# The prologue of a fused attention and gated-product kernel in another order

## The chip, the cores and the metric

One core of one Trainium2 chip runs the kernel. A core has a TensorE (PE: matrix products, into PSUM), a VectorE (DVE), a ScalarE (ACT), a GpSimd (POOL) and a SyncE (SP), each with an instruction queue of its own that it works through in order; SP, ACT and POOL also issue DMA transfers, which run on 16 DMA engines that the core's queues share. The metric is device time in microseconds (us); lower is better. Before the change the median of three runs is 641.73 us (639.29 to 646.2).

## The reference

x has 2048 rows of 576. Everything is bfloat16 at the ends.

```python
mod = (_silu(c) @ w_mod).reshape(c.shape[0], 6, 1, -1)
sa, ca, ga, sb, cb, gb = (mod[:, 0], mod[:, 1], mod[:, 2], mod[:, 3], mod[:, 4], mod[:, 5])
h = _layernorm(x) * (1 + ca) + sa
x = x + ga * A(h, A_wqkv, A_wo)
h = _layernorm(x) * (1 + cb) + sb
x = x + gb * B(h, B_w_gate, B_w_up, B_w_down)
```

A is attention with 32 heads of 18 columns. Row s attends to 8 rows only: s, s-2, ..., s-14 (rows before the first are masked). Its steps are q, k, v = h @ wqkv; 8 logits per row and head; a softmax over these 8; the weighted sum of 8 rows of v; and the product with wo. B is (h @ w_gate) * (h @ w_up) @ w_down with an inner width of 4608.

## The kernel before

The 2048 rows are cut into eight chunks of 256 (CH), each of two tiles of 128 rows (ST = 2, index j). The attention of a chunk i is a list of small pieces, which are Python functions that issue instructions:

- A(i): `a_ln` (layer norm of x, and loads of the next chunks of x), `a_t` (transposes through PE, then scale and shift into hT, by ACT and DVE in turns), five `a_q` (two column tiles of q or k each, products into PSUM, then copied by ACT to qT or kT), two `a_v` (product for v, copied by ACT to v_sb, then stored to vd, a buffer in DRAM, by a DMA that ACT issues, L322).
- B_log(i): eight `b_p` (DVE: q times k shifted by 2w rows, into prod, L341; three buffers) and eight `b_l` (PE: sum per head, into the PSUM tile lg, L351), then `b_sm`, the softmax (DVE, with one exponential on ACT, L367; its result is attn).
- B_av(i): `b_ld` (POOL issues a gather of v's eight shifted copies from vd into vsh, 1.15 MB for a tile of 128 rows, L333), `b_mul` twice per tile (DVE: vsh times attn, L383) and `b_add` (DVE: the sum over the eight, o_sb).
- B_out(i): `b_o` (transposes of o_sb, copied by ACT to oT), `b_w` twice (product pw with wo, L415, then DVE: times ga, plus x), `b_ln`, `b_t` (the second layer norm and its transposes, h2T).

Behind the prologue, `gate_up` and `down` run over five groups of chunks ([0], [1], [2, 3], [4, 5], [6, 7]). The gate and up products (L485, L492) of the first group begin when chunk 0's h2T is there; the attention of the later chunks is spread between them as background pieces.

PE's instructions stay in the order in which the program issues them (`manual_schedule`). The order on DVE, ACT, POOL and SP is chosen by a scheduler at build time, which follows the program's order and priorities; once chosen it is fixed, and each engine waits at its next instruction until its operands are there. Loads on SP and ACT take one of eight semaphores in turn, and a transfer waits at its issue until the one that had the same semaphore has landed.

The prologue before: x's chunk 0, the modulation weights wmA, wqk, wv_raw, x's chunk 1, wmB on SP; c, the four pieces of wo and the zero rows ahead of vd on ACT. Then layer norm 0, the modulation columns for the first norm (pm, written to modc), a reorder of wv's columns by POOL (L558), all of A(0), the loads of wmC and of two blocks of gate and up weights, and

```python
    do(zip_lists(A(1), B_log(0)))
    mod_columns(wmB, 1, True)
    mod_row(wmC, 0, ga_bc)
    mod_row(wmC, 1, gb_bc)
    ...
    do(zip_lists(A2[:7], B_av(0)))
    o0 = B_out(0)
    do(o0[:4], A2[7:], o0[4:])
```

zip_lists takes one piece from each list in turn. The first three blocks of w_down (wd) are loaded by POOL in between.

Of the kernel before, what the change touches and what calls it, by code (L numbers as in the profile page):

```python
# [7 lines left out]
BF = mybir.dt.bfloat16  # L8
# [19 lines left out]
HALO = 16  # L28
# [12 lines left out]
def kernel(  # L41
# [13 lines left out]
    nc = tc.nc  # L55
# [13 lines left out]
    xres = pool("xres", 4)  # L69
# [19 lines left out]
    def ps(shape, dt, name):  # L89
        return psp.tile(shape, dt, name=name, tag="bank")  # L90
# [13 lines left out]
    vd = dramp.tile([HALO + S, D], BF, name="vd")  # L104
# [6 lines left out]
    def load_rows(i, pl, name):  # L111
        ts = []
        for j in range(ST):
            xt = pl.tile([P, D], BF, name=name)
            nc.sync.dma_start(xt[:], x_flat[i * CH + j * P: i * CH + (j + 1) * P, :])
            ts.append(xt)
        return ts

    x_in, x_res = {}, {}

    def load_x(i):
        if i < NCH and i not in x_in:
            x_in[i] = load_rows(i, xin, "x_t")

    def load_res(i):
        x_res[i] = load_rows(i, xres, "x_r")

    wgu_blk, wd_blk = {}, {}
    NG = len(GROUPS)
# [2 lines left out]
    def load_wgu(g):  # L132


        if g >= NG * NBLK or g in wgu_blk:
            return
        cs = slice((g % NBLK) * NB, (g % NBLK + 1) * NB)
        wb = wgup.tile([P, KF, 2, NB], BF, name="wgu")
        wr = wgup.tile([P, NB], BF, name="wgr")
        for t, wsrc in enumerate((B_w_gate, B_w_up)):  # L140
            nc.sync.dma_start(wb[:, :, t, :], wsrc[0:KF * P, cs].rearrange("(k p) n -> p k n", p=P))
            nc.sync.dma_start(wr[64 * t:64 * (t + 1), :], wsrc[KF * P:D, cs])
        wgu_blk[g] = (wb, wr)

    def load_wd(g):
        if g >= NG * NBLK or g in wd_blk:
            return
        r0 = (g % NBLK) * FB * P
        wb = wdp.tile([P, FB, D], BF, name="wd")
        nc.gpsimd.dma_start(wb[:], B_w_down[r0:r0 + FB * P, :].rearrange("(k p) n -> p k n", p=P))  # L150
        wd_blk[g] = wb

    load_x(0)
# [1 line left out]
    sp = sp_guard.__enter__()  # L155
# [6 lines left out]
    def load_wm(blks):  # L162
        wm = sp.tile([P, KT, 2, DP], BF, name="wm", bufs=2)
        nc.gpsimd.memset(wm[:, :, :, D:], 0.0)
        nc.gpsimd.memset(wm[64:, KF, :, :], 0.0)
        for bi, blk in enumerate(blks):
            nc.sync.dma_start(wm[:, 0:KF, bi, 0:D], w_mod[0:KF * P, blk * D:(blk + 1) * D].rearrange("(k p) n -> p k n", p=P))
            nc.sync.dma_start(wm[0:64, KF, bi, 0:D], w_mod[KF * P:D, blk * D:(blk + 1) * D])
        return wm

    wmA = load_wm((0, 1))
    nc.gpsimd.memset(ind[:], 1.0)
    nc.gpsimd.affine_select(out=ind[:], in_=ind[:], compare_op=ALU.is_ge, fill=0.0, base=0,
                            pattern=[[P, KT], [-DH, H]], channel_multiplier=1)
# [9 lines left out]
    nc.gpsimd.memset(wv_raw[64:, KF, :], 0.0)  # L184
    nc.sync.dma_start(wv_raw[:, 0:KF, :], A_wqkv[0:KF * P, 2 * D:3 * D].rearrange("(k p) n -> p k n", p=P))
    nc.sync.dma_start(wv_raw[0:64, KF, :], A_wqkv[KF * P:D, 2 * D:3 * D])
    load_x(1)
    wmB = load_wm((3, 4))
    nc.gpsimd.memset(wo[64:, KF, :], 0.0)
    for dd4 in range(4):  # L190

        nk = (DH - dd4 + 3) // 4
        wsrc = bass.AP(A_wo.tensor, A_wo.offset + dd4 * D, [[DH * D, H], [4 * D, nk], [1, D]])
        nc.scalar.dma_start(wo[dd4 * H:(dd4 + 1) * H, 0:nk, :], wsrc)
    nc.scalar.dma_start(vd[0:HALO, :], wqk[64:64 + HALO, KF, 0, 0:D])


    c_f = sp.tile([P, KT], F32, name="c_f")
    nc.vector.tensor_copy(c_f[:], c_bf[:])
# [8 lines left out]
    def mod_columns(wm, pi, dup):  # L208
        if dup:
            nc.gpsimd.tensor_copy(wm[:, :, :, D:DP], wm[:, :, :, D - 64:D])  # L210
        pm = ps([P, 2, KT], F32, "pm")
        for bi in range(2):
            for m in range(KT):
                for kt in range(KT):
                    nc.tensor.matmul(pm[:, bi, m:m + 1], lhsT=wm[:, kt, bi, m * P:(m + 1) * P],
                                     rhs=sc[:, kt:kt + 1], start=(kt == 0), stop=(kt == KT - 1))
        nc.vector.tensor_copy(modc[:, 2 * pi, :], pm[:, 0, :])
        nc.vector.tensor_scalar_add(modc[:, 2 * pi + 1, :], pm[:, 1, :], 1.0)

# [90 lines left out]
    def a_v(i, j):  # L310
        hT = aa[i]["hT"]
        pv = ps([P, 512], F32, "pv")
        pvr = ps([P, 64], F32, "pvr")
        for kt in range(KT):
            nc.tensor.matmul(pv[:], lhsT=hT[:, kt, j * P:(j + 1) * P], rhs=wv[:, kt, 0:512], start=(kt == 0), stop=(kt == KT - 1))  # L315
        for kt in range(KT):
            nc.tensor.matmul(pvr[:], lhsT=hT[:, kt, j * P:(j + 1) * P], rhs=wv[:, kt, 512:D], start=(kt == 0), stop=(kt == KT - 1))
        v_sb = vstage.tile([P, D], BF, name="v_sb")
        nc.scalar.copy(v_sb[:, 0:512], pv[:])
        nc.scalar.copy(v_sb[:, 512:D], pvr[:])  # L320
        r0 = HALO + i * CH + j * P
        nc.scalar.dma_start(vd[r0:r0 + P, :], v_sb[:])  # L322

    def A(i):
        return ([lambda: a_ln(i), lambda: a_t(i)] + [lambda g=g: a_q(i, g) for g in range(5)]
                + [lambda j=j: a_v(i, j) for j in range(ST)])
# [9 lines left out]
    def b_p(i, w):  # L336

        b = bb.setdefault(i, dict(prod={}, vsh={}))
        off = HALO - DIL * (W - 1 - w)
        prod = prodp.tile([P, KT, CH], BF, name="prod")  # L340
        nc.vector.tensor_tensor(prod[:], aa[i]["qT"][:], aa[i]["kT"][:, :, off:off + CH], ALU.mult)  # L341
        b["prod"][w] = prod

    def b_l(i, w):
        b = bb[i]
        if w == 0:
            b["lg"] = ps([P, ST, W, H], F32, "lg")
        prod = b["prod"].pop(w)
        for j in range(ST):
            for m in range(KT):  # L350
                nc.tensor.matmul(b["lg"][:, j, w, :], lhsT=prod[:, m, j * P:(j + 1) * P], rhs=ind[:, m, :],  # L351
                                 start=(m == 0), stop=(m == KT - 1))
# [23 lines left out]
    def b_ld(i, j):  # L376
        bb[i]["vsh"][j] = b_vsh(i, j)

    def b_mul(i, j, hf):
        b = bb[i]  # L380
        v = b["vsh"][j][:, 4 * hf:4 * hf + 4]
        at = b["attn"][:, j, 4 * hf:4 * hf + 4, None, :].to_broadcast([P, 4, DH, H])
        nc.vector.tensor_tensor(v, v, at, ALU.mult)  # L383
# [52 lines left out]
    def B_log(i):  # L436
        r = [lambda: b_p(i, 0), lambda: b_p(i, 1)]
        for w in range(W):
            r.append(lambda w=w: b_l(i, w))
            if w + 2 < W:  # L440
                r.append(lambda w=w: b_p(i, w + 2))
        return r + [lambda: b_sm(i)]

    def B_av(i):
        r = [lambda: b_ld(i, 0)]
        for j in range(ST):
            if j + 1 < ST:
# [92 lines left out]
    def do(*lists):  # L540
        for ls in lists:
            for piece in ls:
                piece()

    def zip_lists(a, b):
        r = []
        while a or b:
            if a:
                r.append(a.pop(0))
            if b:  # L550
                r.append(b.pop(0))
        return r
# [4 lines left out]
    for kt in range(KT):  # L557
        nc.gpsimd.tensor_copy(wv[:, kt, :].rearrange("p (d h) -> p d h", d=DH),  # L558
                              wv_raw[:, kt, :].rearrange("p (h d) -> p d h", d=DH))
    do(A(0)[1:])  # L560
    nc.vector.tensor_copy(sc_bc[:], sc[:, :, None].to_broadcast([P, KT, P]))
    wmC = load_wm((2, 5))
    load_wgu(0)
    load_wgu(1)
    do(zip_lists(A(1), B_log(0)))
    mod_columns(wmB, 1, True)
    mod_row(wmC, 0, ga_bc)
    mod_row(wmC, 1, gb_bc)
    sp_guard.__exit__(None, None, None)
    hhp = pool("hhp", 1)  # L570
    load_wgu(2)
    for g in range(3):
        load_wd(g)
    A2 = A(2)
    do(zip_lists(A2[:7], B_av(0)))
    o0 = B_out(0)
    do(o0[:4], A2[7:], o0[4:])

    gbg = {0: B_log(1) + B_av(1),
           1: B_av(2) + B_log(3),  # L580
# [40 lines left out]
```

## Time and profile before

| | us |
|---|---|
| median of three runs | 641.73 |
| lowest and highest run | 639.29, 646.2 |
| span of the profiled execution (its own time from first to last instruction) | 640.6 |
| PE busy in it | 576.0 (90%) |
| DVE busy | 303.3 (47%) |
| ACT busy | 283.3 (44%) |
| POOL busy | 77.3 (12%) |
| first gate/up product starts | 81.75 |

The span is one execution, taken by the profiler; it lies within the runs' spread. Matrix products are pipelined, so that PE's busy time isn't PE at its peak. A DMA share near 1 says that all 16 DMA engines had work throughout a stretch. In the lists of transfers the time to landing runs from the issue to the last byte's arrival: in the prologue the two gathers of vsh for chunk 0 took 10.0 and 12.0, the v stores of chunk 0 took 7.0 and 7.5.

### The profile page before, as it was taken

How to read it: one execution, taken by the hardware profiler on the slowest of the kernel's cores; microseconds unless marked ns; L12 is line 12 of the kernel's file. 1: busy time of each engine (PE TensorE's matmuls, PEld its weight loads, DVE VectorE, ACT ScalarE, POOL GpSimd, SP SyncE). 2: the span in 40 equal slices, each digit the busy share in tenths (PEclk: the TensorE clock that was granted, in tenths of full speed). 3: DMA queues.
4: the chain of work that ended last, by engine and by line, in shares of the span. 5: the costliest groups of instructions: out<-in, count | busy, mean ns of one | idle time of the engine just before them, and what ended most of it. 6: DMA issues, size and time to landing. Idle time of an engine off the chain costs nothing.

```text
span 640.6 us, 11591 instructions
## 1 busy us (share of the span) xinstructions
PE 576.0 (90%) x4604; PEld 318.6 (50%) x4672; DVE 303.3 (47%) x632; ACT 283.3 (44%) x582; POOL 77.3 (12%) x128
## 2 busy tenths in 40 slices
PE   1786589989989789999999988999999989999996
PEld 1464267755667556444445654444445543333452
DVE  2547535945944933458385132458393331222103
ACT  2624366551556336455564432455552315555200
POOL 5710200022100222001001210001001110000010
PEclk9988779999999899999999999999999999999999
DMA  9994438886898356545644363446544344441151
GB/s 244 317 376 128 184 117 259 291 280 205 268 344 259 119 182 232 171 134 186 211 144 159 109 224 112 130 148 198 196 136 145 111 150 150 139 138 47 43 150 68
DMA packets 81575, 115.36 MB, mean 180 GB/s; under 512 B 5856, under 2 KB 71664, under 8 KB 81520
## 3 DMA queue, kind: packets, MB, share of 16 engines
q1 hardware_dynamic: 67104, 66.15, 33.2%
q0 software_dynamic: 10832, 45.42, 21.1%
q10 hardware_dynamic: 3584, 3.04, 1.5%
q8 instruction: 36, 0.59, 0.4%
q14 instruction: 19, 0.16, 0.1%
HBM read 109.86 MB, written 4.74 MB: 179 GB/s over the span
## 4 chain that ended last, share of the span: by engine, by line
PE 73%; DVE 10%; DMA 8%; issue 3%; ACT 2%; POOL 2%; SPq 1%; ACTq 0%; POOLq 0%; DVEq 0%
PE pg L492 19%; PE pu L492 18%; PE acc L516 15%; PE pg L485 6%; PE pq L300 4%; PE accr L517 3%; PE pw L415 3%; PE lg L351 2%; DMA wgu<-in_B_w_gate_dram 2%; DMA wgu<-in_B_w_up_dram 2%; PE pv L315 2%; DVE ln_stats L236 2%; DVE vsh L383 2%; DMA wm<-in_w_mod_dram 1%; DVE o_t L534 1%
## 5 line engine op out<-in xcount | busy, mean ns | idle before, releaser
L492 PEld LDWEIGHTS <-wgu 128*128 128x128 bf16 x1440 | 132.3, 98 | 125.8 <-issue 31.6
L492 PE MATMUL pu<-h2T,wgu 128*128 128x512 bf16 (+1 forms) x719 | 154.8, 338 | 1.9 <-DMA wgu<-in_B_w_up_dram 1.8
L492 PE MATMUL pg<-h2T,wgu 128*128 128x512 bf16 (+1 forms) x694 | 152.0, 338 | 3.0 <-issue 2.2
L516 PE MATMUL acc<-wd,hh 128*128 128x512 bf16 x541 | 147.6, 381 | 1.8 <-DMA wd<-in_B_w_down_dram 1.8
L497 ACT CAST g_sb<-pg 128x512 bf16<-128x512 f32 (+1 forms) x180 | 90.0, 500 | 112.1 <-PE pg L492 97.4
L517 PE MATMUL accr<-wd,hh 128*128 128x64 bf16 x576 | 111.1, 193 | 10.7 <-DVE o_t L535 8.7
L499 DVE TENSOR_TENSOR hh<-g_sb,u_sb 128x512 bf16<-128x512 bf16 (+1 forms) x180 | 65.8, 368 | 106.9 <-ACT u_sb L498 106.9
L498 ACT CAST u_sb<-pu 128x512 bf16<-128x512 f32 (+1 forms) x180 | 90.2, 501 | 42.7 <-PE pu L492 36.4
L516 PEld LDWEIGHTS <-hh 128*128 128x128 bf16 x576 | 56.4, 98 | 70.7 <-issue 12.4
L341 DVE TENSOR_TENSOR prod<-qT,kT 128x1280 bf16<-128x1280 bf16 x64 | 52.4, 828 | 53.3 <-PE lg L351 48.2
L300 PE MATMUL pq<-hT,wqk 128*128 128x256 bf16 x400 | 58.0, 292 | 19.2 <-DVE hT L264 9.8
L150 POOL DMA_DIRECT2D wd<-in_B_w_down_dram x45 | 33.9, 754 | 243.9 <-PE accr L517 238.4
L517 PEld LDWEIGHTS <-hh 128*128 128x128 bf16 x576 | 56.4, 98 | 2.6 <-issue 1.9
L300 PEld LDWEIGHTS <-wqk 128*128 128x128 bf16 x400 | 40.2, 104 | 33.4 <-issue 22.0
L485 PE MATMUL pg<-h2T,wgr 64*128 64x512 bf16 (+1 forms) x180 | 46.9, 341 | 1.7 <-ACT h2T L266 1.7
L485 PE MATMUL pu<-h2T,wgr 64*128 64x512 bf16 (+1 forms) x180 | 46.9, 341 | 0.0
L383 DVE TENSOR_TENSOR vsh<-vsh,attn 128x2304 bf16<-128x2304 bf16 x32 | 42.8, 1351 | 0.1
L534 DVE TENSOR_TENSOR o_t<-acc,gb_bc 128x512 bf16<-128x512 f32 x16 | 11.0, 687 | 47.6 <-PE accr L517 45.7
L333 POOL DMA_DIRECT2D vsh<-vd x16 | 14.2, 887 | 156.0 <-DVE o_sb L394 89.4
L264 DVE TENSOR_SCALAR h2T<-tr_pA,modc 128x256 bf16<-128x256 bf16 x16 | 6.6, 410 | 54.3 <-ACT h2T L266 54.3
L351 PEld LDWEIGHTS <-prod 128*128 128x128 bf16 x640 | 23.8, 96 | 9.0 <-DVE prod L341 0.9
L419 DVE TENSOR_TENSOR x<-pw,ga_bc 128x512 bf16<-128x512 f32 x16 | 10.8, 678 | 31.4 <-PE pw L415 31.4
(99 smaller groups left out, 446.1 us busy)
## 6 DMA issues: line engine op xcount, KB each, us to landing
wd<-in_B_w_down_dram POOLq DMA_DIRECT2D x45, 576.0 KB, 4.3
wgu<-in_B_w_gate_dram SPq DMA_DIRECT2D x45, 512.0 KB, 3.8
wgu<-in_B_w_up_dram SPq DMA_DIRECT2D x45, 512.0 KB, 4.9
vsh<-vd POOLq DMA_DIRECT2D x16, 1152.0 KB, 9.2
wm<-in_w_mod_dram SPq DMA_DIRECT2D x6, 576.0 KB, 7.2
wgr<-in_B_w_gate_dram SPq DMA_DIRECT2D x45, 64.0 KB, 3.0
wgr<-in_B_w_up_dram SPq DMA_DIRECT2D x45, 64.0 KB, 2.7
x_t<-in_A_x_dram SPq DMA_DIRECT2D x16, 144.0 KB, 4.3
```

The lines of the kernel that those rows point to most:

```text
L150: nc.gpsimd.dma_start(wb[:], B_w_down[r0:r0 + FB * P, :].rearrange("(k p) n -> p k n", p=P))
L300: nc.tensor.matmul(pq[:, gi, :], lhsT=wqk[:, kt, t, m * P:(m + 1) * P], rhs=hT[:, kt, :], start=(kt == 0), stop=(kt == KT - 1))
L341: nc.vector.tensor_tensor(prod[:], aa[i]["qT"][:], aa[i]["kT"][:, :, off:off + CH], ALU.mult)
L351: nc.tensor.matmul(b["lg"][:, j, w, :], lhsT=prod[:, m, j * P:(j + 1) * P], rhs=ind[:, m, :], start=(m == 0), stop=(m == KT - 1))
L383: nc.vector.tensor_tensor(v, v, at, ALU.mult)
L485: nc.tensor.matmul(pgu[f][t][:, 0:N], lhsT=wr[rows, cs], rhs=ht[rows, KF, 0:N], start=True, stop=False, skip_group_check=True)
L492: nc.tensor.matmul(pgu[f][t][:, 0:N], lhsT=wb[:, k, t, cs], rhs=ht[:, k, 0:N], start=False, stop=(k == KF - 1), skip_group_check=True)
L497: nc.scalar.copy(g[:, 0:N], pg[:, 0:N])
L498: nc.scalar.copy(u[:, 0:N], pu[:, 0:N])
L499: nc.vector.tensor_tensor(hh[:, f, 0:N], g[:, 0:N], u[:, 0:N], ALU.mult)
L516: nc.tensor.matmul(acc[j][:], lhsT=h, rhs=wb[:, f % FB, 0:512], start=(f == 0), stop=(f == FT - 1))
L517: nc.tensor.matmul(accr[:, j, :], lhsT=h, rhs=wb[:, f % FB, 512:D], start=(f == 0 and j == 0), stop=(f == FT - 1), skip_group_check=True)
```

## The change

All of it lies in the prologue; the groups of gate, up and down are left as they are.

- x's chunk 1 is loaded right behind wmA, ahead of wqk. wmB, which was loaded behind x's chunk 1, follows layer norm 1 (and so the loads of x's chunks 2 and 3). wo moves from ACT's queue to SP's, behind wmB; wmC follows wo.
- The zero rows ahead of vd come from a small tile of zeros, stored by SP, and not from wqk's zero part by ACT.
- Chunk 0's logits are put right behind its QKV: the first two b_l between its two a_v, and chunk 1's transposes and its first four a_q between the later b_l. The softmax follows, then the rest of A(1), layer norm 2, and b_mul, b_add of chunk 0, interleaved with chunk 2's transposes and a_q.
- Chunk 0's two v stores are issued by POOL instead of ACT.
- The three first wd blocks are loaded by SP instead of POOL; chunk 0's x for the residual is loaded earlier.
- At the end of the prologue one a_v of chunk 2 stands between b_o and b_w of chunk 0.

```diff
     def load_res(i):
-        x_res[i] = load_rows(i, xres, "x_r")
+        if i not in x_res:
+            x_res[i] = load_rows(i, xres, "x_r")
...
     wmA = load_wm((0, 1))
+    load_x(1)
...
-    load_x(1)
-    wmB = load_wm((3, 4))
     nc.gpsimd.memset(wo[64:, KF, :], 0.0)
-    for dd4 in range(4):
-
-        nk = (DH - dd4 + 3) // 4
-        wsrc = bass.AP(A_wo.tensor, A_wo.offset + dd4 * D, [[DH * D, H], [4 * D, nk], [1, D]])
-        nc.scalar.dma_start(wo[dd4 * H:(dd4 + 1) * H, 0:nk, :], wsrc)
-    nc.scalar.dma_start(vd[0:HALO, :], wqk[64:64 + HALO, KF, 0, 0:D])
-
+
+    def load_wo():
+        for dd4 in range(4):
+
+            nk = (DH - dd4 + 3) // 4
+            wsrc = bass.AP(A_wo.tensor, A_wo.offset + dd4 * D, [[DH * D, H], [4 * D, nk], [1, D]])
+            nc.sync.dma_start(wo[dd4 * H:(dd4 + 1) * H, 0:nk, :], wsrc)
+
+    zrow = sp.tile([HALO, D], BF, name="zrow")
+    nc.gpsimd.memset(zrow[:], 0.0)
+    nc.sync.dma_start(vd[0:HALO, :], zrow[:])
...
-        nc.scalar.dma_start(vd[r0:r0 + P, :], v_sb[:])
+        (nc.gpsimd if i == 0 else nc.scalar).dma_start(vd[r0:r0 + P, :], v_sb[:])
...
-    do(A(0)[1:])
+    A0, A1, A2 = A(0), A(1), A(2)
+    do(A0[1:7])
+    A1[0]()
+    wmB = load_wm((3, 4))
     nc.vector.tensor_copy(sc_bc[:], sc[:, :, None].to_broadcast([P, KT, P]))
+    L, PR = (lambda w: b_l(0, w)), (lambda w: b_p(0, w))
+    PR(0)
+    PR(1)
+    A0[7]()
+    L(0)
+    PR(2)
+    A0[8]()
+    b_ld(0, 0)
+    b_ld(0, 1)
+    for w, piece in ((1, None), (2, A1[1]), (3, None), (4, A1[2]), (5, A1[3]), (6, A1[4]), (7, A1[5])):
+        L(w)
+        if w + 2 < W:
+            PR(w + 2)
+        if piece:
+            piece()
+    b_sm(0)
+    load_wo()
     wmC = load_wm((2, 5))
+    do(A1[6:])
+    A2[0]()
+    load_res(0)
+    av = [lambda j=j, k=k: (b_mul(0, j, k) if k < 2 else b_add(0, j)) for j in range(ST) for k in range(3)]
+    av[0]()
     load_wgu(0)
     load_wgu(1)
-    do(zip_lists(A(1), B_log(0)))
     mod_columns(wmB, 1, True)
+    av[1]()
     mod_row(wmC, 0, ga_bc)
     mod_row(wmC, 1, gb_bc)
     sp_guard.__exit__(None, None, None)
     hhp = pool("hhp", 1)
     load_wgu(2)
+    do(zip_lists(av[2:], A2[1:7]))
     for g in range(3):
-        load_wd(g)
-    A2 = A(2)
-    do(zip_lists(A2[:7], B_av(0)))
+        load_wd(g, nc.sync)
     o0 = B_out(0)
-    do(o0[:4], A2[7:], o0[4:])
+    do(o0[:1], A2[7:8], o0[1:4], A2[8:], o0[4:])
```

(load_wd has a new parameter for the queue that issues it, GpSimd by default.)

More of the change, by code (lines that the diff above doesn't have):

```diff
@@ L143, in load_wgu, with load_wd @@
         wgu_blk[g] = (wb, wr)
-    def load_wd(g):
+    def load_wd(g, queue=nc.gpsimd):
         if g >= NG * NBLK or g in wd_blk:
@@ L149, in load_wd @@
         wb = wdp.tile([P, FB, D], BF, name="wd")
-        nc.gpsimd.dma_start(wb[:], B_w_down[r0:r0 + FB * P, :].rearrange("(k p) n -> p k n", p=P))
+        queue.dma_start(wb[:], B_w_down[r0:r0 + FB * P, :].rearrange("(k p) n -> p k n", p=P))
         wd_blk[g] = wb
```

## The prediction

> **What bounds the kernel now.** I read the page first: TensorE (PE) is busy 90% of the span, its gaps lie almost all in the first 82 us. The stage table shows that, each row being a stretch, the busy time of each engine (instruction counts in brackets), the granted PE clock, the busy share of the DMA engines and their rate:
>
> ```profile
> core 0: us, PE busy (x) PEld busy (x) DVE busy (x) ACT busy (x) POOL busy (x), PEclk, DMA share, GB/s
> 0.00:10.00 10.00, 0.00 (x0) 0.10 (x1) 2.40 (x9) 1.28 (x1) 8.79 (x20) 1.00 0.82 198
> ...
> 50.00:60.00 10.00, 5.58 (x39) 3.67 (x37) 6.90 (x9) 3.89 (x9) 0.00 (x0) 0.84 0.46 144
> 60.00:70.00 10.00, 5.99 (x46) 4.25 (x46) 6.34 (x8) 3.69 (x7) 3.73 (x5) 0.84 0.24 90
> ```
>
> Behind the prologue PE works 527.39 of 558 us, and the change leaves that part's instructions alone. So the question is one number: when the gate/up product (L485) starts. Then the timeline of the first 90 us (start, duration, engine line, idle time before it and what ended it):
>
> ```profile
> 12.39 0.21 ACT L201 ACTIVATE e_f<-c_f 128x5 f32<-128x5 f32 x1 [10.30 <-DMA wm<-in_w_mod_dram]
> ...
> 18.08 5.80 POOL L558 COPY wv<-wv_raw 128x576 bf16<-128x576 bf16 x5 [8.18 <-DMA wv_raw<-in_A_wqkv_dram]
> ...
> 19.89 6.62 PE L300 MATMUL pq<-hT,wqk 128*128 128x256 bf16 x47 [2.06 <-DVE hT L264]
> ...
> 27.23 2.48 DVE L341 TENSOR_TENSOR prod<-qT,kT 128x1280 bf16<-128x1280 bf16 x3 [1.16 <-ACT ln_rstd L240]
> ...
> 35.63 0.90 POOL L333 DMA_DIRECT2D vsh<-vd  x1 [5.38 <-DMA vd<-v_sb]
> ...
> 53.07 1.03 DVE L369 TENSOR_REDUCE ssum<-dd 128x64 f32<-128x512 f32 x1 [3.75 <-ACT dd L367]
> ...
> 56.48 3.89 DVE L383 TENSOR_TENSOR vsh<-vsh,attn 128x2304 bf16<-128x2304 bf16 x3
> 56.62 6.96 PE L300 MATMUL pq<-hT,wqk 128*128 128x256 bf16 x47 [0.18 <-DVE hT L264]
> ...
> 66.43 0.56 PE L405 MATMUL oT_pA<-ident,o_sb 128*128 128x128 bf16 x7 [0.93 <-DVE o_sb L394]
> ...
> 81.75 0.37 PE L485 MATMUL pg<-h2T,wgr 64*128 64x256 bf16 x1 [1.71 <-ACT h2T L266]
> ```
>
> To be seen: ScalarE (ACT) idles 10.30 us at the start, its queue standing behind the wo and vd transfers; chunk 0's softmax is late (3.75 us of it behind ACT, which stands at L322 until 48.12 and 51.11); the DMA engines are full from 10 to 50 us (share 1.06 to 1.09); the attention multiply L383 starts at 56.48 with both vsh tiles long there (issued 35.63 and 37.79, landed after 10.0 and 12.0).
>
> **The change, step by step.** All starts of the new kernel are estimates from these rows.
>
> *Start.* wo's four issues and vd's zero rows leave ACT, so e_f goes at about 5.6 and sc, which came 0.84 behind e_f (12.39 to 13.23), at 6.5. The modulation product waits for wmA instead: it landed at 11.9 beside 0.66 MB of wo; without it at 8.3 to 9.5 (1.6 MB at the 200 to 320 GB/s of these stretches). But DVE now has chunk 1's statistics (2.0 us and the small steps, x1 landing at 9 to 10) ahead of the modc copies: these come at 12 to 13 in place of 14.80, and ACT puts chunk 1's two ln_xn (0.87 each) among the hT steps. QKV of chunk 0 runs at full rate from about 15.3, not 19.89, and ends at 22, not 26.5. The zero rows' transfer on SP (18 KB) costs one issue, 0.5 us, under full DMA queues: nothing.
>
> *That gain is stopped at once.* kT's copies on ACT now stand behind chunk 2's ln_xn, which waits for a POOL memset, and POOL has the five wv copies ahead of it. wv_raw landed at 18.0 to 18.4; with 0.39 MB less ahead of it (wo and so on out, x1 in) 1.2 us earlier: 16.9 + 5.8 + 1.16 (wm memset) + 0.2 = 24.1, less up to 0.8 if the queue runs better. Then ACT needs 0.87 + 0.58 + 0.87 + 0.58: kT is whole at 26 to 27; I take 26.3, against 27.2. So logits start 0.9 us earlier, not 4.5.
>
> *Logits and softmax.* First product at 27.1. PE: lg 0.41, pv 1.35, two lg, transposes 0.8, two lg: 31.3; 1.6 for hT (it stood 1.78 there before); three pq groups of 1.4 and three lg: 38.3, where before lg ended at 45.5. Softmax: 0.83 + 1.01 + 0.69 + 0.64 + 1.03 + 0.54 + 0.68 = 5.4, two products of chunk 1 that are put between 1.6, handovers 0.6: attn at 46.0, against 56.1. ACT's exponential is ahead of the v stores here, so the 3.75 us go.
>
> *The added wait.* Chunk 0's two v stores move from ACT to POOL. Its order is: store 0, the wmB copy (wmB landed long before, at about 25), vsh0 (waits for store 0), **store 1**, vsh1 (waits for store 1). Store 1 is queued behind vsh0's wait, and its data behind vsh0's 1.15 MB on the same queue; in the old kernel both stores were out at 30.0. ACT's v_sb of chunk 1 waits for store 1 too, with ga_bc, gb_bc and chunk 2's hT behind it; those are not needed before 50.
> Prices: a store issued at 28.36 landed after 7.0, at 48.12 after 5.6, at 76 after 1.7 with idle queues. POOL's queue goes in order: wd landed at 33.8, 35.9, 38.0, then vsh0 7.6 us later and vsh1 4.2 later. Store 0: kT copy to 27.2, v_sb, issue 27.5, landed 32.5 to 35. vsh0 issued 33.5 to 36, landing 8.6 to 9.5 later (0.9 issue, some 1 to start, 7.6): 42 to 45. Store 1 lands 0.5 to 1.5 behind it. vsh1: 0.9 + 1 + 4.2 to 7.6: 48.5 to 56. I take 52, since SP's loads still run until about 50 and the full-queue rows are the nearest.
>
> The Trainium skill ("DMA: Bandwidth & Descriptors", section "Issuing engine by pattern") speaks against this move: a simple store belongs on Sync, and GpSimd's software path is the slower one. Its section on the anatomy of a software DMA gives about 2.0 us plus bytes over 436 GB/s, an estimate of 2.3 for a store and 4.7 for vsh; the chain would then end near 44 and bind nothing, and the sum would be that of the faster rival below. The full queues of this trace (7.0 us for such a store) decide otherwise.
>
> *What it moves.* Call T the start of the third multiply (vsh1's first). DVE's own chain allows 46.0 + 2 x 1.27 + 0.3 = 48.8; vsh1 makes it 52. DVE now has chunk 2's two hT steps behind it: 1.27 + 1.27 + 0.41 + 0.67 + 0.41 = 4.1, so chunk 2's QKV starts at T + 4.1 and not 56.6; 7.0 us to T + 11.1, where o_sb is ready (T + 8.9). Transposes 1.0, ACT's oT copies 1.4 with pv(2,0) on PE in their shade, pw's two big groups 4.1 (68.50 to 72.6): T + 17.6. From there to L485 it was 81.75 - 72.6 = 9.15 and stays so. Gate/up starts at T + 26.75: with 52 at 78.75, 3.0 us earlier. Old kernel by the same steps: QKV at 56.6, oT 2.8 us late for o_sb; that wait goes, too, and is in the sum.
>
> wd through SP and load_res earlier: nothing; wd is read first by the down product some 50 us after gate/up starts, under SP's queue. If that cover went, one wd is 8 us. The bank that lg holds makes the fourth pq group wait for dd, 1 us, in PE's slack.
>
> The profiled execution's span is 640.6, the median of the runs 641.73: 1.1 lies around it or is scatter (639.29 to 646.2). 640.6 - 3.0 + 1.1 = 638.7. With vsh1 at 48.8 to 56 (T), 635.5 to 642.7.
>
> **Rivals.** *Faster:* the stores don't bind, because store 1 isn't held up by vsh0 or the queues are emptier than I think (idle prices 1.7 and 5.6 us). Then DVE binds at T = 48.8: 6.2 us, 635.5; with kT whole 2 us earlier as well, 633.5. For it: SP has fewer transfers in flight at 28 to 33. Against: the share of 1.07 there. *Slower:* the store chain at full-queue prices throughout: store 0 at 28.4 + 7.5 = 35.9, vsh0 at +12.0 = 47.9, store 1 at 49.4, vsh1 at +12.0 = 61.4: gate/up at 88.2, 6.5 later, 648.2. It decides as soon as vsh1 lands after 55; a landing at 58.5 gives 645.2. For it: the 12.0 was measured; against: that was behind vsh0 in the queue. *No net change:* the gain at L485 is lost at 110 to 127 us, where the chain of waits runs over DVE's attention of chunk 1: 641.7; against it, that work is counted from gate/up's start and two more of its products are done ahead. A prologue that isn't reordered at all can be left out: the order of instructions on each engine of the built program shows it.
>
> A cold PE in the wait before chunk 2's QKV: the clock was 0.84 there and 512-column products took 0.43 us from 46 to 73, so that price is in the rows already.
>
> **How the numbers follow.** Forecast 0.52 (635.5 to 642.7), faster rival 0.20, slower 0.21, no net change 0.07. Some 1% (6.4 us) is what a measurement of this kernel can tell from no change. Faster by more, under 635.3: nearly all of the first rival's share, 0.19. Slower by more, over 648.1: the upper end of the slower one, with what I haven't seen, 0.13. Within: 0.68. The range 634.0 to 646.5 leaves out some 0.08 below and 0.11 above.
>
> **What would show it.** Right: first pm near 9, QKV 0 from 15, L341 near 26, attn near 46, POOL's second store behind vsh0, the third L383 near 52 waiting for DMA vsh, chunk 2's QKV some 4 us behind it, L485 (L489 there) near 79. Wrong: the third L383 following the second without a gap (faster rival), or beginning after 55 (slower one); stages behind gate/up with another length.

## The result and the profile after

The changed kernel takes 635.12 us (median of four runs, 633.44 to 637.32), the old one beside it 641.81 (639.29 to 646.2): a ratio of 0.9887 with a 95% interval of 0.9843 to 0.9931. The time lies in the predicted range (634.0 to 646.5), 0.4 below the 635.5 at which the forecast's own part of it begins. The profiled execution's span is 632.6, against 640.6. One run of experiment 3 below, at a granted clock of 0.56, took 982.35 us and is left out there.

Gate/up starts at 72.68 and not at 81.75, so the prologue is 9.07 us shorter; forecast were 3.0. Behind it the kernel takes 559.9 in place of 558.9. The stage table of the changed kernel, in the stretches that were shown of the old one:

```profile
core 0: us, PE busy (x) PEld busy (x) DVE busy (x) ACT busy (x) POOL busy (x), PEclk, DMA share, GB/s
0.00:10.00 10.00, 1.60 (x43) 1.48 (x44) 4.03 (x15) 3.41 (x6) 8.32 (x22) 1.00 0.81 218
50.00:60.00 10.00, 8.04 (x53) 6.01 (x53) 7.51 (x11) 2.97 (x6) 1.77 (x2) 0.66 1.07 364
60.00:70.00 10.00, 5.61 (x50) 3.04 (x48) 5.96 (x21) 4.88 (x11) 0.78 (x4) 1.00 0.52 175
```

PE works in the first 10 us now (it did not before). From 60 to 70 it has its full clock, where the old kernel had 0.84; from 50 to 60 it has less, 0.66 against 0.84. The timeline of the changed kernel (start, duration, engine line, idle time before it and what ended it):

```profile
5.94 0.21 ACT L205 ACTIVATE e_f<-c_f 128x5 f32<-128x5 f32 x1 [3.85 <-DVE ln_rstd L243]
...
14.99 7.58 PE L304 MATMUL pq<-hT,wqk 128*128 128x256 bf16 x48 [0.39 <-ACT hT L270]
...
15.97 5.82 POOL L562 COPY wv<-wv_raw 128x576 bf16<-128x576 bf16 x5 [3.73 <-DMA wv_raw<-in_A_wqkv_dram]
...
21.44 0.37 DVE L247 SCALAR_TENSOR_TENSOR ln_nmr<-ln_mv,ln_rstd 128x2 f32<-128x2 f32 x1 [1.94 <-ACT ln_rstd L245]
...
21.89 0.87 ACT L252 ACTIVATE ln_xn<-x_t,ln_nmr,ln_rstd 128x576 bf16<-128x576 bf16 x1 [0.48 <-DVE ln_nmr L247]
...
23.07 0.21 POOL L250 MEMSET ln_xn<- 128x128 bf16 x1
...
24.57 5.14 DVE L345 TENSOR_TENSOR prod<-qT,kT 128x1280 bf16<-128x1280 bf16 x6 [2.77 <-ACT kT L309]
...
25.39 0.70 POOL L326 DMA_DIRECT2D vd<-v_sb  x1 [0.61 <-ACT v_sb L324]
...
32.08 0.91 POOL L337 DMA_DIRECT2D vsh<-vd  x1 [5.26 <-DMA vd<-v_sb]
...
32.97 0.57 POOL L326 DMA_DIRECT2D vd<-v_sb  x1
...
38.28 1.05 DVE L373 TENSOR_REDUCE ssum<-dd 128x64 f32<-128x512 f32 x1 [0.69 <-ACT dd L371]
...
40.20 0.90 POOL L337 DMA_DIRECT2D vsh<-vd  x1 [6.66 <-DMA vd<-v_sb]
...
48.66 1.36 DVE L387 TENSOR_TENSOR vsh<-vsh,attn 128x2304 bf16<-128x2304 bf16 x1 [4.01 <-DMA vsh<-vd]
...
52.26 7.71 PE L304 MATMUL pq<-hT,wqk 128*128 128x256 bf16 x48 [0.23 <-ACT hT L270]
...
61.59 1.24 PE L419 MATMUL pw<-wo,oT 128*128 128x512 bf16 x5
...
72.68 0.37 PE L489 MATMUL pg<-h2T,wgr 64*128 64x256 bf16 x1 [1.34 <-ACT h2T L270]
```

To be seen, in order: ACT's late start is gone; QKV of chunk 0 ends at 22.6 and not at 26.5; the softmax's sum waits 0.69 for ACT and not 3.75. Then the new wait: POOL's second v store goes out at 32.97, behind vsh's first gather, although the first store had gone at 25.39; vsh's second gather can be issued only at 40.20, when that store has landed (6.9 us), and the third attention multiply waits 4.01 us for it.

### The profile page after: what moved, and what is told of

It reads as the page before. It is cut to its first block, busy times and chain, and to the rows that moved or that the text cites. A ratio compares the mean times of both kernels' runs of the same rounds, so it can differ in the third digit from the quotient of the medians.

```text
span 632.6 us, 11592 instructions
## 1 busy us (share of the span) xinstructions
PE 574.2 (91%) x4604; PEld 318.3 (50%) x4672; DVE 304.4 (48%) x632; ACT 283.5 (45%) x582; POOL 74.6 (12%) x128
## 3 DMA queue, kind: packets, MB, share of 16 engines
HBM read 109.86 MB, written 4.74 MB: 181 GB/s over the span
## 4 chain that ended last, share of the span: by engine, by line
PE 77%; DVE 10%; DMA 7%; ACT 2%; issue 2%; SPq 1%; POOL 0%; ACTq 0%; DVEq 0%; POOLq 0%
PE pg L496 19%; PE pu L496 18%; PE acc L520 16%; PE pq L304 6%; PE pg L489 6%; PE accr L521 3%; DVE ln_stats L240 2%; PE pw L419 2%; DMA vd<-v_sb 2%; PE lg L355 2%; DMA wgu<-in_B_w_up_dram 2%; PE pv L319 2%; DMA vsh<-vd 1%; ACT ln_xn L252 1%; DVE o_t L538 1%
## 5 line engine op out<-in xcount | busy, mean ns | idle before, releaser
L151 POOL DMA_DIRECT2D wd<-in_B_w_down_dram x42 | 31.6, 752 | 245.9 <-PE accr L521 240.4
L355 PEld LDWEIGHTS <-prod 128*128 128x128 bf16 x640 | 23.9, 96 | 10.4 <-DVE prod L345 2.5
L355 PE MATMUL lg<-ind,prod 128*128 128x32 bf16 x640 | 25.3, 176 | 2.1 <-DVE prod L345 2.1
```

The lines of the kernel that those rows point to most:

```text
L151: queue.dma_start(wb[:], B_w_down[r0:r0 + FB * P, :].rearrange("(k p) n -> p k n", p=P))
```

## The experiments

Times of gate/up's start and of QKV's full rate are from the profiled execution, as are the spans; ratios are of runs to runs of the old kernel on the same chip.

| kernel | QKV 0 at full rate | waits for vsh | gate/up | span | ratio (95% interval) |
|---|---|---|---|---|---|
| before | 19.89 | 0 | 81.75 | 640.6 | 1 |
| after | 14.99 | 4.01 | 72.68 | 632.6 | 0.9887 (0.9843 to 0.9931) |
| 1: stores on ACT | 15.44 | 0 | 69.48 | 628.2 | 0.9794 (0.9772 to 0.9815) |
| 2: wd on POOL | 15.28 | 2.95 + 1.76 | 72.53 | 633.0 | 0.9872 (0.9854 to 0.9890) |
| 3: old order of the end | 15.24 | 5.23 | 72.51 | 633.3 | 0.9892 (0.9867 to 0.9917) |
| 4: only wo and zero rows moved | 13.09 | 0 | 74.33 | 635.0 | 0.9870 (0.9850 to 0.9890) |
| 5: wo back on ACT | 21.41 | 0.55 + 2.95 | 74.88 | 633.2 | 0.9895 (0.9870 to 0.9919) |
| 6: before, chunk 1's stores on POOL | 19.65 | 0 | 78.69 | 638.2 | 0.9958 (0.9940 to 0.9975) |
| 7: second store on ACT | 15.06 | 0 | 69.80 | 628.6 | 0.9815 (0.9792 to 0.9839) |
| 8: as 1, hT early | 15.62 | 0 | 67.73 | 627.6 | 0.9793 (0.9767 to 0.9819) |
| 9: old load order | 13.20 | 0 | 69.45 | 627.9 | 0.9814 (0.9789 to 0.9839) |
| 10: before, wgu later | 19.80 | 0 | 80.81 | 640.2 | 1.0006 (0.9987 to 1.0024) |
| 11: as 1, wo back on ACT | 20.79 | 0 | 72.16 | 630.4 | 0.9835 (0.9811 to 0.9859) |
| 12: 1, 8 and 9 together | 13.10 | 0 | 66.63 | 628.9 | 0.9809 (0.9773 to 0.9845) |

My first theory was that the change gains at the start and in the logits, and gives part of it back to the v stores on POOL; the first rival, that the whole gain is ACT's queue, freed of wo.

**1. Chunk 0's v stores back on ACT.**

```diff
-        (nc.gpsimd if i == 0 else nc.scalar).dma_start(vd[r0:r0 + P, :], v_sb[:])
+        nc.scalar.dma_start(vd[r0:r0 + P, :], v_sb[:])
```

> The new kernel with chunk 0's two v stores back on ACT's queue; nothing else is changed. My theory: in the new kernel the third attention multiply waits for vsh1 (idle 4.01 us, starts at 48.66), because store 1 stands behind vsh0 on POOL. With both stores out on ACT at 25 and 28, vsh1 streams right behind vsh0 and lands at 43 to 46; DVE's own chain allows the third multiply at 44.6. Gate/up starts 24 us behind it, at 69 to 70 in place of 72.7; span 629 to 630. Rival: ACT stands at the second store for a semaphore, as it did before the change, hT of chunk 1 is late, and the gain is eaten: gate/up at 72 to 75, span 632 to 635.

Measured: 629.85 us (628.75 to 631.82), gate/up at 69.48. POOL and DVE of this kernel:

```profile
30.34 1.03 POOL L337 DMA_DIRECT2D vsh<-vd  x1 [3.46 <-DMA vd<-v_sb]
33.24 0.88 POOL L337 DMA_DIRECT2D vsh<-vd  x1 [1.88 <-DMA vd<-v_sb]
...
43.18 1.36 DVE L387 TENSOR_TENSOR vsh<-vsh,attn 128x2304 bf16<-128x2304 bf16 x1
44.53 2.62 DVE L387 TENSOR_TENSOR vsh<-vsh,attn 128x2304 bf16<-128x2304 bf16 x2
```

The second gather goes out 7.0 us earlier, none of the four multiplies waits for a gather, and gate/up comes 3.2 us earlier. The move of the stores is a loss inside a change that gains.

**2. wd's loads back on POOL.**

```diff
     for g in range(3):
-        load_wd(g, nc.sync)
+        load_wd(g)
```

> The new kernel with the first three wd loads back on POOL. They then stand ahead of the v stores and of vsh0 on POOL's queue, and both stores ahead of vsh0. My theory (POOL's queue works in order): 1.7 MB more ahead of vsh0, which lands at 42 to 44 and not 39.4, but store 1 no longer waits for it, vsh1 lands at 46.5 to 48.5: third multiply there, span 630.5 to 632.6, no slower than the new kernel. Rival (loads on different queues only share the rate, the order doesn't matter): vsh0 at 39 to 40 and vsh1 at 44 to 45, span 629. Second rival (wd on SP is what made the change pay): vsh1 after 51, span over 635.

Measured: 634.73 us, gate/up at 72.53. POOL's order changed with it (two wd blocks ahead of the first store, the third between the two stores, both gathers behind them); the gathers went at 35.17 and 37.79, and now the first multiply waits 2.95 and the third 1.76, and the third comes at 49.15, later than the theory had it. At the end it makes no difference, but two effects cancel: the second store no longer stands behind a gather, and wd's 1.7 MB now stand ahead of both. What wd's place is worth by itself this run does not show.

**3. The old order at the prologue's end.**

```diff
-    do(o0[:1], A2[7:8], o0[1:4], A2[8:], o0[4:])
+    do(o0[:4], A2[7:], o0[4:])
```

> The new kernel with the old order at the prologue's end (pv(2,0) behind pw and not between oT and pw). My theory: PE idles 1.2 to 1.5 us for ACT's oT copies, pw starts at the same 61.6 to 61.8, and the chain behind it is the same: no difference, span within 0.6 of 632.6. Rival: without pv in the gap the PE clock falls back and pw's ten 512-column products take 0.43 us each instead of 0.22: 1.7 to 2 us longer, span 634.5.

Measured: gate/up at 72.51, the median 635.71, the interval of the ratio on top of the changed kernel's. PE idles 1.03 us ahead of pw, and the granted clock is 1.00 all the same (from 61.5 to 64.1). From the transposes to pw it takes 1.76 us, from pw to gate/up 11.10; in the changed kernel 1.78 and 11.09. The product that was put between costs or gains nothing that can be seen.

**4. Only wo and the zero rows moved**, in the old kernel.

```diff
-        nc.scalar.dma_start(wo[dd4 * H:(dd4 + 1) * H, 0:nk, :], wsrc)
-    nc.scalar.dma_start(vd[0:HALO, :], wqk[64:64 + HALO, KF, 0, 0:D])
+        nc.sync.dma_start(wo[dd4 * H:(dd4 + 1) * H, 0:nk, :], wsrc)
+    zrow = sp.tile([HALO, D], BF, name="zrow")
+    nc.gpsimd.memset(zrow[:], 0.0)
+    nc.sync.dma_start(vd[0:HALO, :], zrow[:])
```

> The kernel before with one part of the change: wo's loads and the zero rows on SP and not on ACT. My theory: the start gains (first modulation product at 7 to 9 in place of 13.3, QKV of chunk 0 ends at 21 to 22 in place of 26.5), but the logits stay zipped with chunk 1's QKV and ACT's exponential stays behind the v stores; gate/up starts 2 to 4 us earlier than before, span 636.5 to 638.5. Rival 1: the ACT queue was all of it, span 632 to 634. Rival 2: the start is hidden by the vsh transfers behind wd on POOL, span 640 to 641.

Measured: 635.7 us, gate/up at 74.33: this part alone brings 7.42 of the 9.07 us, far more than I had expected. Besides the start, ACT's standstill at chunk 1's v stores (48.12 and 51.11 in the old kernel) is gone:

```profile
38.16 0.33 ACTq L324 DMA_DIRECT2D vd<-v_sb  x1
39.31 0.33 ACTq L324 DMA_DIRECT2D vd<-v_sb  x1
44.32 0.64 ACT L369 ACTIVATE dd<-dd 128x512 f32<-128x512 f32 x1
```

The exponential went at 52.39 before; here it goes at 44.32. The rival stood: the queue move seemed to be nearly all. Runs 5, 6 and 11 ask how much of it is the start, how much the standstill, and what the reordered logits then bring at all.

**5. The complement: all of the change, but wo and the zero rows on ACT as before.**

```diff
-    def load_wo():
-        for dd4 in range(4):
...
-            nc.sync.dma_start(wo[dd4 * H:(dd4 + 1) * H, 0:nk, :], wsrc)
...
+    for dd4 in range(4):
...
+        nc.scalar.dma_start(wo[dd4 * H:(dd4 + 1) * H, 0:nk, :], wsrc)
+    nc.scalar.dma_start(vd[0:HALO, :], wqk[64:64 + HALO, KF, 0, 0:D])
```

> The changed kernel with wo's four transfers and the zero rows back on ACT's queue at their old place; logits, loads and stores stay as changed. Theory (the queue move carries nearly all of the gain, the reordered logits about 1 to 2 us of it once chunk 0's stores sit on POOL): e_f goes near 12.4 again in place of 5.9, QKV of chunk 0 at full rate near 19 to 20 in place of 15.0, and gate/up starts at 76 to 79 in place of 72.7; span 636.5 to 639. Rival (the reordered logits carry the gain by themselves, the start is absorbed by the store chain on POOL): gate/up within 1 us of 72.7, span 632 to 634. Second rival (both parts are needed, neither gives anything alone): gate/up at 81 to 82, span 640 to 641.

Measured: 636.54 us, gate/up at 74.88, between the theory and its first rival. QKV starts 6.4 us later than in the changed kernel, even 1.5 later than before, and yet only 2.2 us are lost at gate/up. So each half alone brings about 7 us (7.42 and 6.87) and both together 9.07: 5.2 us are counted twice. The two are not clean halves, for POOL's order changed here, too: both stores (30.11 and 32.19) go ahead of both gathers (35.50 and 37.49), so that the changed kernel's wait is not in this run.

**6. The old kernel with only chunk 1's v stores on POOL.**

```diff
-        nc.scalar.dma_start(vd[r0:r0 + P, :], v_sb[:])
+        (nc.gpsimd if i == 1 else nc.scalar).dma_start(vd[r0:r0 + P, :], v_sb[:])
```

> The old kernel with chunk 1's two v stores on POOL's queue, behind vsh0, vsh1 and the kT copy; wo and the zero rows stay on ACT. It takes away only ACT's late standstill behind those stores (exp at 52.39 though dd was ready at 48.58), not the late start. Theory (the queue move of wo gains in two places, 5 us at the start and 3.8 at the exponential, and they are the same us counted in one chain): exp near 48.7, attn near 52.5, gate/up 2 to 3.5 us earlier than 81.75, so at 78.3 to 79.8, span 637 to 638.5. Rival (the standstill is harmless, since vsh, QKV2 or o_sb bind there anyway): gate/up within 1 us of 81.75 and span 640 to 641.

Measured: 640.38 us (639.49 to 642.12), gate/up at 78.69 as the theory had it; the exponential goes at 49.88 and attn is done at 53.60, each some 1.1 later than it said, with the first product of the logits 1.04 later than in the old kernel (28.27 against 27.23). Without the standstill gate/up comes 3.06 us earlier, and each half of the change removes it: the exponential goes at 44.32 in run 4 and at 41.19 in run 5. By difference, 4.36 of run 4's gain are left for the start; no run moves the start and keeps the standstill.

**7. Only chunk 0's second store back on ACT.**

```diff
-        (nc.gpsimd if i == 0 else nc.scalar).dma_start(vd[r0:r0 + P, :], v_sb[:])
+        (nc.gpsimd if i == 0 and j == 0 else nc.scalar).dma_start(vd[r0:r0 + P, :], v_sb[:])
```

> The changed kernel with chunk 0's second v store alone put back on ACT's queue; the first stays on POOL. Theory (what the stores on POOL cost is that the second one lands behind vsh0 in POOL's queue): the second store lands before vsh0 does, vsh1 is issued right behind vsh0 and lands 43 to 46, the third attention multiply starts at 45.8 to 46.5 without a wait for a DMA and gate/up at 69.5 to 70.3, as with both stores on ACT (69.48); span 628 to 629. Rival (POOL as such is the slower queue, either store costs by its issue there): gate/up about half way, 70.8 to 71.8, the first multiply late for vsh0 in place of the third; span 630 to 631.5.

Measured: 631.0 us, gate/up at 69.80, within 0.3 of run 1. The first store may stay on POOL: what costs is the second one's place behind the gather.

**8. Run 1 with chunk 2's transposes ahead of the modulation columns.**

```diff
     load_wgu(1)
+    A2[1]()
     mod_columns(wmB, 1, True)
...
-    do(zip_lists(av[2:], A2[1:7]))
+    do(zip_lists(av[2:], A2[2:7]))
```

> The changed kernel with both stores of chunk 0 on ACT and, besides, chunk 2's transposes and hT written ahead of the modulation columns of the second half (DVE then has hT between the multiplies and not behind them). Theory (with the stores out of the way, QKV of chunk 2 waits 2.7 us for hT behind DVE's multiplies, and that is the next link): PE's wait before QKV of chunk 2 falls under 1 us, gate/up at 68 to 68.6 in place of 69.48, span 626.5 to 627.5. Rival (DVE's o_sb binds the tail, so earlier hT only delays the multiplies): gate/up 69.2 to 70, span 628 to 629.

Measured: gate/up at 67.73, 1.75 earlier than in run 1, PE's longest wait ahead of QKV 2 falls from 2.72 to 0.86, the span is 627.6. The mechanism held, and gave 0.3 more than the theory's range. In the runs nothing of it is to be seen (629.86 against 629.85): behind gate/up this execution took 559.9 us, run 1's 558.7.

**9. The old place of x's chunk 1 and wmB among the loads.**

```diff
     wmA = load_wm((0, 1))
-    load_x(1)
...
+    load_x(1)
+    wmB = load_wm((3, 4))
     nc.gpsimd.memset(wo[64:, KF, :], 0.0)
...
     A1[0]()
-    wmB = load_wm((3, 4))
```

> The changed kernel with the loads of x's chunk 1 and of wmB back in the old place (x1 and wmB behind wv); all else as changed. Theory (this part pays nothing by itself): QKV of chunk 0 at full rate within 1 us of 15.0, kT within 1 us of 24.5, gate/up within 1 us of 72.7, span 631.6 to 633.6. Rival (x1 loaded early is what lets chunk 1's transposes stand among the logits): wv_raw lands 1 us earlier but chunk 1's hT comes late, the logits end 2 us or more behind 35.0 and gate/up goes to 74.5 or later, span 634.5 or more.

Measured: 631.35 us, gate/up at 69.45. Neither held: I had said that this part pays nothing, and undoing it wins 3.2 us. POOL's timeline shows through what:

```profile
25.87 0.70 POOL L327 DMA_DIRECT2D vd<-v_sb  x1
29.01 0.55 POOL L327 DMA_DIRECT2D vd<-v_sb  x1 [2.44 <-ACT v_sb L325]
31.61 0.91 POOL L338 DMA_DIRECT2D vsh<-vd  x1 [2.05 <-DMA vd<-v_sb]
33.97 0.89 POOL L338 DMA_DIRECT2D vsh<-vd  x1 [1.46 <-DMA vd<-v_sb]
```

Both stores are on POOL as in the changed kernel, but the scheduler has put the second one ahead of the first gather. QKV's earlier start (13.20) gains nothing by itself: the first product is at 24.49, against 24.57, and POOL's copies of wv begin at 16.03, against 15.97. With run 7 this settles the place of the loss: it is neither POOL nor the load order, but the second store behind the gather's wait.

**10. The old kernel with the first two gate/up blocks asked for later.**

```diff
-    load_wgu(0)
-    load_wgu(1)
     do(zip_lists(A(1), B_log(0)))
+    load_wgu(0)
+    load_wgu(1)
```

> The old kernel with nothing moved but the first two blocks of gate/up weights (load_wgu(0) and load_wgu(1)), which are asked for behind chunk 1's QKV and the logits. Theory (ACT's standstill at chunk 1's v stores, until 48.12 and 51.11, is a wait for a semaphore that the store shares with a transfer of SP: the gate/up weights issued at 35.36 and 39.12 landed at 48.06 and 51.02, 12.7 and 11.9 us later): the two stores go 0.1 us behind their v_sb copies, at about 42.6 and 43.9, the exponential at 48.7 to 50, attn near 53 in place of 56.1, gate/up 2.5 to 3.5 us earlier at 78.2 to 79.3; span 637 to 638.2, like the run with chunk 1's stores on POOL (638.2). Rival (the stores wait for vsh or for room in the full DMA queues): they stay within 1 us of 48.1 and 51.1, or move with vsh's landing, and gate/up stays within 1 us of 81.75.

Measured: 642.5 us, gate/up at 80.81, the ratio 1.0006. The gain that I expected did not come, but the semaphore was the right one. In the built program of the old kernel the two stores of chunk 1 and two of SP's loads stand so (the other semaphores are left out):

```
ACT  L322 vd<-v_sb (chunk 1, first)          waits DMAHW0   the last before it: SP L142 wgr<-in_B_w_up_dram
ACT  L322 vd<-v_sb (chunk 1, second)         waits DMAHW3   the last before it: SP L141 wgu<-in_B_w_gate_dram
```

In the old kernel's profile these two loads (the answer for their tiles: times in ns, then the start; below each the time to landing) are

```profile
L142 SPq DMA_DIRECT2D wgr<-in_B_w_up_dram x1: 471/471/471, 35.4 to 35.4; - x1
DMA to landing us min/median/max: 12.7/12.7/12.7
...
L141 SPq DMA_DIRECT2D wgu<-in_B_w_gate_dram x1: 480/480/480, 39.1 to 39.1; - x1
DMA to landing us min/median/max: 11.9/11.9/11.9
```

and its timeline has ACT's stores and exponential at

```profile
48.12 0.33 ACTq L322 DMA_DIRECT2D vd<-v_sb  x1
51.11 0.33 ACTq L322 DMA_DIRECT2D vd<-v_sb  x1
52.39 0.64 ACT L367 ACTIVATE dd<-dd 128x512 f32<-128x512 f32 x1
```

35.36 + 12.7 = 48.06, and the store goes at 48.12; 39.12 + 11.9 = 51.02, and the second goes at 51.11. In run 10 the two stores share their semaphores with the loads in the same two places of SP's row. The second of these, and ACT:

```profile
L141 SPq DMA_DIRECT2D wgu<-in_B_w_gate_dram x1: 376/376/376, 37.8 to 37.8; - x1
DMA to landing us min/median/max: 13.3/13.3/13.3
```

```profile
43.14 0.33 ACTq L322 DMA_DIRECT2D vd<-v_sb  x1
51.19 0.33 ACTq L322 DMA_DIRECT2D vd<-v_sb  x1
52.46 0.64 ACT L367 ACTIVATE dd<-dd 128x512 f32<-128x512 f32 x1
```

The first store's load had landed, so it goes at once; the second's was issued at 37.81 and landed 13.3 later, at 51.11, and ACT goes on at 51.19. One of two standstills remained, and with it the late exponential. A wait for vsh or for room in the full queues would have held the first store, too. ACT's late start has the same cause: in the old kernel's program the transfer of the zero rows, which goes at 11.92, waits for a semaphore that it shares with the last transfer of wmA, issued at 4.35 and landed 7.5 later, at 11.85.

**11. Run 1 with wo and the zero rows on ACT.** The edits of runs 1 and 5 together.

> The changed kernel with wo's transfers and the zero rows back on ACT (late start, QKV of chunk 0 at full rate near 21) and chunk 0's v stores back on ACT: the reordered logits and loads alone. Theory (the reordering is worth the most, and in the run with wo on ACT it lost 2.95 us to vsh behind the POOL stores): the third attention multiply follows without a wait near 48.7, gate/up at 71.8 to 73, span 630 to 631.5, under the changed kernel's 632.6. Rival (with the late start the stores on ACT are late themselves, or stand behind a load's semaphore): gate/up at 74 to 76, span 633 to 635, no better than with the stores on POOL (74.88, 633.2).

Measured: 632.54 us (630.56 to 633.5), gate/up at 72.16, as the theory had it. The reordered logits and loads alone, with the stores left where they were, bring 9.59 us at gate/up, more than the whole change; the intervals of the two ratios overlap. One of ACT's stores of chunk 1 still stands some 2 us behind a load (46.53), but the exponential (41.65) is ahead of it. With the stores on ACT throughout, run 4's 7.42 and these 9.59 stand against run 1's 12.27: 4.74 are counted twice, and the standstill by run 6 makes 3.06 of them. What the rest is no run isolates.

**12. Runs 1, 8 and 9 together.**

> The changed kernel with chunk 0's stores on ACT, chunk 2's transposes ahead of the modulation columns, and the loads of x's chunk 1 and wmB in the old place, all three together. Theory (what the start gains stops at kT, whose copies came at 24.4 to 25.5 in all runs with an early start, so the earlier QKV of the old load order, 13.2 in place of 15.0, is worth nothing at the end; hT early is worth 1.7 us at gate/up): gate/up at 67.2 to 68.2 as in the run with hT early (67.73), span 627 to 628. Rival (the 1.8 us at the start come through, since kT's copies no longer stand behind chunk 2's ln_xn): gate/up at 65.9 to 66.5, span 625.5 to 626.5.

Measured: 630.67 us (628.32 to 633.02), gate/up at 66.63, the earliest of all and next to the rival's range: QKV starts 2.5 us earlier than in run 8, the first product 1.6 (24.06 against 25.68), gate/up 1.1. POOL's copies of wv start 1.45 earlier (15.61 against 17.06), so that the 1.6 need not be QKV's. The span of 628.9 is longer than run 8's all the same. Behind gate/up this execution took 562.3 us, run 8's 559.9. The stage tables of both, counted from gate/up's start (30, 30 and 60 us), first run 12, then run 8:

```profile
66.63:96.63 30.00, 29.86 (x320) 22.33 (x319) 13.71 (x33) 18.58 (x49) 0.00 (x0) 0.94 0.66 204
96.63:126.63 30.00, 27.68 (x232) 18.60 (x234) 21.69 (x52) 16.78 (x43) 4.18 (x8) 0.94 0.90 297
126.63:186.63 60.00, 56.85 (x602) 39.60 (x605) 33.90 (x66) 26.89 (x73) 7.29 (x10) 0.97 0.82 255
```

```profile
67.73:97.73 30.00, 29.86 (x310) 21.77 (x310) 12.56 (x32) 17.53 (x46) 0.00 (x0) 0.90 0.63 200
97.73:127.73 30.00, 27.84 (x251) 19.13 (x250) 22.86 (x54) 17.45 (x45) 4.17 (x8) 1.00 0.89 300
127.73:187.73 60.00, 56.94 (x627) 40.05 (x625) 34.51 (x68) 28.19 (x77) 7.26 (x10) 1.00 0.84 263
```

PE is as busy, but from 97 to 187 us its granted clock is 0.94 and 0.97 in place of 1.00, and it gets through fewer products. Why the clock was lower in that execution stays open. Runs 1, 8, 9 and 12 cannot be told apart by their medians (629.85 to 631.35); the intervals of runs 1, 8 and 9 end below the changed kernel's, which begins at 0.9843, and run 12's ends at 0.9845.

## Why the prediction was right, and where it was not

The range held the time, and the wait that the prediction put in the middle of its working, the second store behind the gather on POOL, is there and is worth what it says: taking it away gains 3.2 us (run 1), 2.9 (run 7), 3.2 (run 9). But the sum at gate/up was short by 6.1 us, in two terms: T, the third multiply, came at 48.66 and not at 52 (3.3), and from T to gate/up it took 24.0 and not 26.75 (2.7). That the time lies in the range all the same is partly luck: 641.73 less the 9.07 at gate/up would have been 632.7, below it. Behind gate/up the profiled execution took 1.07 longer, and the runs' medians lie 6.7 apart where the profiled spans lie 8.0 apart.

- *Start*: right. e_f 5.94 (5.6 was said), modc 12.85 (12 to 13), QKV at full rate 14.99 (15.3), its end 22.57 (22).
- *"That gain is stopped at once"*: it is, and by POOL's copies of wv, but not through the wait that was named; this step failed. The prediction had ACT's copies of kT wait, through chunk 2's ln_xn, for a POOL memset behind wv's copies, and so kT whole at 26.3. ACT's ln_xn ran at 21.89, ahead of that memset (23.07), for which the built program has no wait there, and kT was whole at 24.47. What the ln_xn waited for (0.48 us) is DVE's ln_nmr. That small instruction took 0.16 us at 12.77; here it took 0.37 and ended at 21.81, when the last of wv's copies ended (21.79). In run 1 it took 0.83 and ended at 22.64, the copies at 22.63; in run 8 it took 1.10 and ended at 22.91, the copies at 22.90. From its end ACT needs 2.66 us for the two ln_xn and the last two copies of kT, in these three kernels alike (kT whole at 24.47, 25.30 and 25.58). So an earlier QKV gains little while wv is copied: in runs 9 and 12, with QKV at full rate 1.8 and 1.9 us earlier still, the first product is at 24.49 and 24.06. That ln_nmr lasts until a copy on POOL ends is read from these times; no run here took the copies away, or shows why. The sizes: wv's copies began at 15.97 (16.9 was said), and the 1.36 us of memsets are not in the chain.
- *Logits and softmax*: right in its parts. 10.4 us from the first product to the last logit (11.2 was said), 6.9 more until attn is done (7.7); with kT 1.8 earlier, attn is there at 41.9 and not at 46.0.
- *The added wait*: the mechanism right, the sizes at the short end. Store 0 issued at 25.39, landed after 6.4; vsh0 issued at 32.08, landed after 7.3; store 1 landed 0.5 behind it; vsh1 issued at 40.20, landed after 8.4, at 48.6. The first gather was quicker than the 8.6 to 9.5 that were said, the others lie in their ranges. From store 0's issue to T it took 23.3 us (24.5 was said), and the chain began 2.1 earlier, because kT did: together the 3.3.
- *The tail*: mis-sized. The transposes at T + 11.15 (11.1 was said) come right by two errors that cancel: QKV 2 is at T + 3.6 and not 4.1 (the terms given for that add up to 4.03), and it takes 7.55 us and not 7.0, at a granted clock of 0.50 from 51.6 to 56. From the transposes to pw it takes 1.8 us and not 2.4, pw's two groups take 2.47 and not 4.1, and the layer norm behind them 8.6 and not 9.15. (The old kernel's rows give 4.3 and 8.9 for these two, since pw ends there at 72.81 and not at 72.6; their sum is the same.) The prediction took the cold clock to be "in the rows already"; but the rows' clock is not the changed kernel's. In the old kernel PE had three gaps (1.69, 0.93 and 1.39 us) between QKV 2 and pw, and the granted clock from 66.4 to 73 was 0.55; in the changed one QKV 2 runs straight into the transposes and the clock from 61.5 to 64.1 is 1.00. Two rows of the old kernel's timeline and its stretch, then the changed kernel's stretch:

```profile
65.27 0.23 PE L405 MATMUL oT_pA<-ident,o_sb 128*128 128x128 bf16 x1 [1.69 <-DVE o_sb L394]
68.50 1.91 PE L415 MATMUL pw<-wo,oT 128*128 128x512 bf16 x4 [1.39 <-ACT oT L407]
66.40:73.00 6.60, 5.18 (x29) 2.65 (x31) 1.43 (x4) 1.29 (x2) 1.65 (x4) 0.55 0.82 318
```

```profile
61.50:64.10 2.60, 2.60 (x27) 1.42 (x26) 1.19 (x3) 0.89 (x4) 0.00 (x0) 1.00 0.80 289
```

- *The rivals*: the faster rival named the time (635.5) but not the reason, for its condition was that the stores don't bind, and they do; that case is run 1, at 629.85. The slower one failed on the price of vsh1: 12.0 us was that of a gather queued behind another, and here the queue was empty ahead of it. "No net change" fell: of the 9.07 us only 1.07 is lost behind gate/up in the profiled executions, and over all fourteen kernels that part took 558.2 to 562.3.
- *What was not priced*: ACT's standstill at chunk 1's stores was in the rows, and taken as 3.75 us that go; that wo's removal alone would take it away too was not worked out. That, by runs 4, 5 and 6, is part of why the two halves of the change do not add up (7.42 and 6.87 against 9.07): 3.06 of the 5.2 us. The forecast let the store chain swallow the start and gave 3.0 us for the whole change; the moved queue alone brings 7.42 (run 4).

The Trainium skill ("DMA: Bandwidth & Descriptors", section "Issuing engine by pattern") has a simple store issued by Sync rather than GpSimd. No run here has the stores on Sync. Run 1, with them on ScalarE, is 3.2 us ahead of the changed kernel at gate/up; but run 9, with both stores on GpSimd and no gather between them, is as good as run 1, so the price here was the order in the queue. By its section on the anatomy of one software DMA the estimate for a store was 2.3 us; measured were 6.4 and 6.9, beside full DMA queues.

On the clock, the Trainium skill ("TensorE: Matmul & The Clock Gate", section "Why this matters for your kernels") asks for no gap in PE's work of more than about 3 us. Run 4, with a wait of 3.36 us between QKV 2 and the transposes, had a granted clock of 0.50 from 60 to 66 us; run 8, with one of 2.05, had 1.00 from 56 to 60. That agrees. Run 9 does not: after a wait of 2.75 us ahead of QKV 2 it had 0.50 from 48.6 to 52, and the old kernel's three gaps, none over 1.7 us, were followed by 0.55.

```profile
48.09 0.37 PE L305 MATMUL pq<-hT,wqk 128*128 128x256 bf16 x1 [2.75 <-DVE hT L269]
48.60:52.00 3.40, 3.24 (x15) 2.11 (x15) 3.40 (x6) 0.62 (x2) 0.88 (x1) 0.50 1.05 308
```

(The first line is run 9's timeline, the second its stretch.) No run changed a gap and nothing else, so that the gaps set the clock is argued from these rows, and at what length they do stays open.

## What to carry to other kernels

Price a queue move by what stands behind the moved instruction and by which semaphore it takes its turn on: here one queue was late twice, and two different edits removed the same second wait, which is part of why their gains did not add. A transfer that depends on nothing should not stand, in an in-order queue, behind one that waits; look in the built program where the scheduler put it, since an edit elsewhere can move it (run 9). When waits go or come, the clock of the products behind them can be another one (pw 0.55 before and 1.00 after, QKV 2 0.50 after a wait of 6.94 us); a row's duration is taken over with the clock that it had. And ask of a small instruction on the chain what its length was elsewhere: ln_nmr's 0.37 to 1.10 us in place of 0.16 was a wait that no idle time shows.

## What the runs showed of the hardware that was not expected

- Transfers with full queues: SP's loads of 64 and 512 KB took 12.7, 11.9 and 13.3 us to land (issued at 35.36 and 39.12 in the old kernel, at 37.81 in run 10), the v stores of chunk 0 (144 KB) 7.0 and 7.5 in the old and 6.4 and 6.9 in the changed kernel; a store of that size at 76.59 in the old kernel, with the DMA engines busy to 0.29 (76 to 79), took 1.7.
- A gather of 1.15 MB landed after 7.3 and 8.4 us with nothing ahead of it in POOL's queue (the changed kernel), and after 10.0 and 12.0 with wd's three blocks and the other gather ahead (the old one).
- With the gaps gone, ten products of pw (with their ten small ones) took 2.47 us at a granted clock of 1.00, against 4.3 at 0.55.
- DVE's ln_nmr (128x2) lasted until a copy of wv on POOL ended: 0.37 us to 21.81 (the copy to 21.79), 0.83 to 22.64 (22.63), 1.10 to 22.91 (22.90) in the changed kernel and runs 1 and 8; 0.16 where POOL did not copy.
